# A gated recurrence and a feed-forward on one core: TensorE's order written by hand, the recurrence one step ahead, first pairs turned on TensorE, the square on ScalarE

## The chip, the cores and the metric

One core of a Trainium2 chip. The metric is the device time of one execution in microseconds. A time is the median of a kernel's runs. A ratio is the mean time of one kernel's fast runs over the mean of the kernel before's fast runs in the same rounds, so it is not quite the ratio of the medians quoted beside it. The kernel before has 946.0 us (943.6 to 948.8, 3 runs), its profiled execution a span of 942.1 us.

## The reference, cut to what matters

```python
def _attn_ref(q, k, v, a_re, a_im):          # each 4 x 8 x 768 x 48
    mag = np.sqrt(a_re * a_re + a_im * a_im)
    scale = np.minimum(mag, 0.999) / (mag + 1e-06)
    a_re_n, a_im_n = (a_re * scale, a_im * scale)
    for t in range(S):
        ...                                   # complex state S, decayed by a at each t
        S_re, S_im = (new_re + kv, new_im)
        y[:, :, t] = np.einsum('bhd,bhde->bhe', q[:, :, t], S_re)
    return y

def _moe_ref(x, w_in, w_out):                 # 3072 x 384, 384 x 2048, 2048 x 384
    h = x @ w_in
    g = h * (1.0 / (1.0 + np.exp(-h)))
    return (g @ w_out).astype(np.float32)
```

The recurrence is done in 24 chunks of 128 time steps, two chunks (a pair) at a time: 12 pairs. Within a chunk, decays and phases are prefix sums, q and k are rotated by them, and one masked product of q and k gives attention weights. Each pair then goes through the feed-forward: eight *hidden* steps (12 matrix products each) and eight *result* steps (8 each). The feed-forward's weights arrive as pairs of 32-bit words, from which the kernel rebuilds fp32 values, piece by piece.

Some words used below. A *hole* is time in which TensorE stands. The *carry* is the last phase of the chunk before, added to the first row of a chunk's phases. *Gates* are the decays and phases made from `a_re` and `a_im`; a *burst* is a run of ScalarE functions of one kind for them (logarithms, or sines and arctangents, or exponentials), opened by a table load of 1.28 us. *Gating* is VectorE's product (L420) that follows ScalarE's tanh after a hidden step. The *front* is the time in which weights are still being rebuilt, the *steady part* what follows.

## The kernel before

The parts that matter: the rebuilding of a piece of weights, the making of the phases, and the order. A list of work for the recurrence, one for the gates ahead and one for the feed-forward are merged evenly, and a scheduler then chooses each engine's order within that.

```python
    def load_w(dst, parts):                 # one piece: 512 columns of w_in, 384 of w_out
        ...                                 # x, t, u: scratch tiles; lo, hi: the raw words
        nc.gpsimd.tensor_tensor(out=x, in0=hi.bitcast(F32), in1=hi.bitcast(F32), op=ALU.mult)
        nc.vector.tensor_scalar(out=t, in0=hi, scalar1=3, ...)
        nc.vector.scalar_tensor_tensor(out=t, in0=hi, scalar=-0x40000000, in1=t, ...)
        ...                                 # four more VectorE operations; the last writes dst

    def phases(n):
        ...
        if place(n)[1] > 0:
            carry = att.tile([1, DM], F32, tag="carry", name=f"carry{n}", bufs=1)
            nc.sync.dma_start(out=carry, in_=X[before(n)]["turn"][C - 1:C])
            nc.gpsimd.tensor_tensor(out=th[0:1], in0=th[0:1], in1=carry, op=ALU.add)
        ps = p_m.tile([C, DM], F32, tag="m", name=f"phase{n}")
        nc.tensor.matmul(ps, lhsT=upto, rhs=th, start=True, stop=True)
        ...

    def turned(n):                          # q and k to head-dimension-first
        ...
        nc.vector.transpose(sq, ...)        # 32x32 blocks
        for b in range(NB):
            for a in range(NA):
                nc.sync.dma_start(out=x["T"][ts(b, Q), :, a], in_=sq[ts(a, Q), b])
        ...

    for p in range(NP + 1):
        lists = []
        if p < NP:
            lists += [attention(p), ahead(p)]
        if p == 0:
            lists.append([... all pieces of w_in ...] + [... all pieces of w_out ...])
        else:
            lists.append(feed(p - 1))
        merge(*lists)
```

## Time and profile before

| What | Before |
|---|---|
| Median time, span of the profiled run | 946.0 us, 942.1 us |
| Mean granted TensorE clock in it | 0.856 |
| TensorE busy up to 300 us | 135.6 us |
| Start of the first attention weights, of the first result step | 60.6 us, 185.6 us |

The page of the kernel before has the engines' busy times in its first part and, in its fifth, the costliest groups (columns: line, engine, operation, tile; busy us and mean ns of one; idle us of the engine just before them and what ended most of it):

```profile
PE 702.8 (75%) x3424; PEld 518.6 (55%) x3424; DVE 431.4 (46%) x587; ACT 264.2 (28%) x409; POOL 161.5 (17%) x144
...
L398 PE MATMUL o<-w,g 128*128 128x384 f32 x768 | 283.4, 515 | 16.1 <-DVE g L388 16.1
...
L321 PE MATMUL a<-T 96*128 96x128 f32 x384 | 57.8, 301 | 74.7 <-DMA T<-sq 74.7
L254 PE MATMUL phase<-th,upto 128*128 128x384 f32 x48 | 31.2, 755 | 99.4 <-POOL th L252 63.9
```

TensorE is the busiest engine but stands for a quarter of the span. It stands at two places above all: 75 us at attention weights, for turned q and k, and 99 us at the phase sums, mostly for the carry that GpSimd adds.

### The profile page before, as it was taken

How to read it: one execution, taken by the hardware profiler on the slowest of the kernel's cores; microseconds unless marked ns; L12 is line 12 of the kernel's file. 1: busy time of each engine (PE TensorE's matmuls, PEld its weight loads, DVE VectorE, ACT ScalarE, POOL GpSimd, SP SyncE). 2: the span in 40 equal slices, each digit the busy share in tenths (PEclk: the TensorE clock that was granted, in tenths of full speed). 3: DMA queues.
4: the chain of work that ended last, by engine and by line, in shares of the span. 5: the costliest groups of instructions: out<-in, count | busy, mean ns of one | idle time of the engine just before them, and what ended most of it. 6: DMA issues, size and time to landing. Idle time of an engine off the chain costs nothing.

```text
span 942.1 us, 9656 instructions
## 1 busy us (share of the span) xinstructions
PE 702.8 (75%) x3424; PEld 518.6 (55%) x3424; DVE 431.4 (46%) x587; ACT 264.2 (28%) x409; POOL 161.5 (17%) x144
## 2 busy tenths in 40 slices
PE   0333002855988979969979939979979859999997
PEld 0133001643765756746757727757757637777675
DVE  2856998896335244264362153362362252331110
ACT  5641000142161260251341251341521341311111
POOL 1411222232022031040040040040120040100000
PEclk9655555886997978989979969979979969999999
DMA  9335346744224313422602632612532522222000
GB/s 141 71 65 102 91 115 138 172 113 73 43 48 67 71 35 50 87 37 35 111 10 44 113 60 36 110 17 39 92 45 37 95 44 51 37 50 39 3 17 20
DMA packets 309592, 61.83 MB, mean 66 GB/s; under 512 B 300552, under 2 KB 305952, under 8 KB 309536
## 3 DMA queue, kind: packets, MB, share of 16 engines
q1 hardware_dynamic: 309536, 61.14, 35.3%
q8 instruction: 29, 0.48, 0.2%
q14 instruction: 27, 0.22, 0.1%
HBM read 36.25 MB, written 4.76 MB: 44 GB/s over the span
## 4 chain that ended last, share of the span: by engine, by line
PE 57%; DVE 12%; ACT 12%; SPq 5%; issue 5%; POOL 4%; DMA 3%; DVEq 0%; POOLq 0%; ACTq 0%
PE o L398 25%; PE h L383 22%; ACT mag L192 3%; ACT s L192 3%; ACT L189 3%; PE a L321 2%; POOL mag L222 2%; PE s L366 2%; SPq L312 2%; PE y L341 2%; DVE qk L298 2%; ACT cs L192 2%; DVE t L151 2%; PE phase L254 1%; PE y L344 1%
## 5 line engine op out<-in xcount | busy, mean ns | idle before, releaser
L398 PE MATMUL o<-w,g 128*128 128x384 f32 x768 | 283.4, 515 | 16.1 <-DVE g L388 16.1
L383 PE MATMUL h<-xT,w 128*128 128x256 f32 x1152 | 264.6, 381 | 3.1 <-DMA xT<-y 3.1
L383 PEld LDWEIGHTS h<-xT,w 128*128 128x128 f32 x1152 | 217.0, 191 | 46.3 <-issue 8.0
L398 PEld LDWEIGHTS o<-w,g 128*128 128x128 f32 x768 | 152.8, 201 | 119.0 <-DVE g L388 25.7
L388 DVE SCALAR_TENSOR_TENSOR g<-tanh,h 128x512 f32<-128x512 f32 x96 | 65.7, 684 | 253.1 <-ACT tanh L192 253.1
L192 ACT ACTIVATE tanh<-h 128x512 f32<-128x512 f32 x96 | 56.1, 594 | 383.3 <-PE h L383 374.2
L321 PE MATMUL a<-T 96*128 96x128 f32 x384 | 57.8, 301 | 74.7 <-DMA T<-sq 74.7
L254 PE MATMUL phase<-th,upto 128*128 128x384 f32 x48 | 31.2, 755 | 99.4 <-POOL th L252 63.9
L321 PEld LDWEIGHTS a<-T 96*128 96x128 f32 x384 | 55.4, 214 | 84.2 <-issue 61.3
L254 PEld LDWEIGHTS phase<-th,upto 128*128 128x128 f32 x48 | 11.3, 270 | 103.6 <-POOL th L252 65.7
L350 ACT COPY xT<-y 128x384 f32<-128x384 f32 x24 | 11.4, 475 | 175.1 <-PE y L341 107.3
L372 POOL TENSOR_TENSOR S<-S,decs 96x384 f32<-96x384 f32 x16 | 13.2, 825 | 273.4 <-DVE S L371 212.0
L325 DVE TENSOR_TENSOR w<-a,upto 128x512 f32<-128x512 f32 x48 | 32.3, 681 | 59.1 <-PE a L321 59.1
L366 PE MATMUL s<-v,qk 128*96 128x48 f32 x320 | 38.3, 281 | 26.6 <-ACT y L352 18.3
L366 PEld LDWEIGHTS s<-v,qk 128*96 128x96 f32 x320 | 37.1, 198 | 32.2 <-ACT y L352 19.7
L222 POOL TENSOR_TENSOR mag<-mag,s 128x768 f32<-128x768 f32 x12 | 25.2, 2100 | 163.8 <-DVE s L202 151.1
L341 PE MATMUL y<-w,v 128*64 128x128 f32 (+1 forms) x384 | 42.2, 294 | 13.1 <-DVE w L325 13.1
L189 ACT ACT_TABLE_LOAD x37 | 47.5, 1283 | 1.4 <-PEq L620 0.8
L148 POOL TENSOR_TENSOR x<-raw 128x384 f32<-128x384 f32 (+1 forms) x28 | 27.7, 988 | 99.2 <-DVE w L159 69.1
L192 ACT ACTIVATE mag<-mag 128x768 f32<-128x768 f32 x36 | 30.2, 838 | 46.9 <-POOL mag L222 46.0
L308 DVE STREAM_TRANSPOSE sq<-qk 128x1536 f32<-128x1536 f32 x24 | 42.4, 1766 | 2.1 <-DMA T<-sq 2.1
L298 DVE TENSOR_TENSOR qk<-ek,cs 128x768 f32<-128x768 f32 x24 | 38.0, 1582 | 9.6 <-POOL ek L296 9.6
(51 smaller groups left out, 613.2 us busy)
## 6 DMA issues: line engine op xcount, KB each, us to landing
T<-sq SPq DMA_DIRECT2D x288, 64.0 KB
raw<-in_moe_w_out_dram SPq DMA_DIRECT2D x16, 384.0 KB
re<-in_a_re_dram SPq DMA_DIRECT2D x24, 192.0 KB
im<-in_a_im_dram SPq DMA_DIRECT2D x24, 192.0 KB
k<-in_k_dram SPq DMA_DIRECT2D x24, 192.0 KB
q<-in_q_dram SPq DMA_DIRECT2D x24, 192.0 KB
v<-in_v_dram SPq DMA_DIRECT2D x24, 192.0 KB
raw<-in_moe_w_in_dram SPq DMA_DIRECT2D x24, 192.0 KB
```

What stands on the lines that cost most here:

```text
L189: chain(nc.scalar.preload_act_table_set(name))
L192: chain(nc.scalar.activation(out=out, in_=in_, func=func, **kw))
L222: nc.gpsimd.tensor_tensor(out=mag, in0=mag, in1=s1, op=ALU.add)
L254: nc.tensor.matmul(ps, lhsT=upto, rhs=th, start=True, stop=True)
L298: nc.vector.tensor_tensor(out=x["qk"][:, w], in0=heads(e).unsqueeze(2).to_broadcast([C, H, 2, D]), in1=x["cs"], op=ALU.mult)
L308: nc.vector.transpose(sq, x["qk"].rearrange("p w h c d -> p (w h) (c d)").rearrange("p g (b i) -> p b g i", i=Q))
L321: nc.tensor.matmul(ps[:, h], lhsT=x["kT"][:, hh * HH + h], rhs=x["qT"][:, hh * HH + h], start=True, stop=True)
L341: nc.tensor.matmul(to, lhsT=v_[:, cols], rhs=x["w", h // HH][:, h % HH], start=True, stop=not carried)
L366: nc.tensor.matmul(ps[:, h], lhsT=x["qk"][:, 1, h].rearrange("p c d -> p (c d)"), rhs=x["v"][:, h], start=True, stop=True)
L383: nc.tensor.matmul(ps[:, ji], lhsT=w1[:, dc, ts(jp * 2 + ji, C)], rhs=A[p]["xT"][:, dc], start=(dc == 0), stop=(dc == ND - 1))
L388: nc.vector.scalar_tensor_tensor(out=g, in0=th, scalar=1.0, in1=ps, op0=ALU.add, op1=ALU.mult)
L398: nc.tensor.matmul(A[p]["o"][m], lhsT=A[p]["g", jp][:, ji, ts(m, C)], rhs=w2[:, j], start=(j == 0), stop=(j == NJ - 1))
```

## The change

Its intent: fill TensorE's holes. The square leaves GpSimd. The first two pairs' q and k are turned by TensorE and need no transfers. While weights are still being rebuilt, two feed-forwards run side by side, so that each new piece is used twice. And after the front every pair's phase sums are issued a whole step before they are needed. All of TensorE's instructions stand in the order in which the program names them. Smaller parts came with it: a third buffer for raw words, the first loads of q, k and v issued by ScalarE, the first pair's gates in halves, and the PSUM buffers shared in another way.

```diff
-        nc.gpsimd.tensor_tensor(out=x, in0=hi.bitcast(F32), in1=hi.bitcast(F32), op=ALU.mult)
+        nc.scalar.activation(out=x, in_=hi.bitcast(F32), func=AF.Square)
@@ gates: the first pair in halves, on VectorE
+        helper = nc.vector if split else nc.gpsimd
@@ rotated
-            nc.gpsimd.tensor_tensor(out=e, in0=x[name].rearrange("p h d -> p (h d)"), in1=e,
-                                    op=ALU.mult)
+            (nc.vector if n < EARLY else nc.gpsimd).tensor_tensor(
+                out=e, in0=x[w].rearrange("p h d -> p (h d)"), in1=e, op=ALU.mult)
@@ turned
+        if n < EARLY:
+            for g in range(4):
+                w, hh = divmod(g, 2)
+                ps = p_o.tile([D2, HH, C], F32, tag="o", name=f"tp{n}_{g}")
+                for h in range(HH):
+                    nc.tensor.transpose(
+                        ps[:, h],
+                        x["kq"[w] + "r"][:, hh * HH + h].rearrange("p c d -> p (c d)"), ident)
+                nc.scalar.copy(out=T[:, ts(g, HH)], in_=ps)
@@ PSUM: weights, output, state and sums share two buffers
-    p_a = fast.enter_context(tc.tile_pool(name="p_a", bufs=2, space=PSUM))
-    p_o = fast.enter_context(tc.tile_pool(name="p_o", bufs=2, space=PSUM))
+    p_o = fast.enter_context(tc.tile_pool(name="p_o", bufs=4, space=PSUM))
@@ order of the pieces of weights (1: w_in, 2: w_out)
+    conv = [(1, s, lambda s=s, dc=dc: load_w1(s, dc)) for s in range(2) for dc in range(ND)]
+    for s in range(4):
+        conv += [(2, j // 2, lambda j=j: load_w2(j)) for j in range(4 * s, 4 * s + 4)]
+        if s < 2:
+            conv += [(1, s + 2, lambda s=s, dc=dc: load_w1(s + 2, dc)) for dc in range(ND)]
@@ the order: h(p), r(p) are hidden and result steps of pair p
+    with tc.manual_schedule(engines={mybir.EngineType.PE}):
+        angles(0, True)
+        both(phases, 0)
+        ... (the front, some 110 lines, by hand)
+        for p in range(3, NP + 1):
+            step(p, parts(hidden, p - 1), parts(result, p - 1))
@@ the steady step, cut
+    def step(p, h, r):
+        ...
+        h(1)
+        if ahead:
+            both(phases, p + 1)
+        h(1)
+        ...
+        weights(2 * p, 0); weights(2 * p, 1)
+        r(1)
+        state(2 * p); output(2 * p)
+        ...
+        trig_burst(p + 1)
+        ...
```

## The prediction

> **What bounds the kernel now.** I read the busy digits first, then busy time by stretch, TensorE's waits, and last the chain of waits. The digits (a slice is 23.6 us):
>
> ```profile
> span 942.1 us, 9656 instructions
> ...
> PE   0333002855988979969979939979979859999997
> ...
> DVE  2856998896335244264362153362362252331110
> ...
> PEclk9655555886997978989979969979979969999999
> ```
>
> In slices 3 to 6 VectorE reads 6 to 9 while TensorE reads 0 to 3 at half clock. From slice 11 TensorE reads 9, with a dip about every third slice. Busy time by stretch (columns: length; busy us and count of PE, PEld, DVE, ACT, POOL; clock, DMA share, GB/s):
>
> ```profile
> 80.00:120.00 40.00, 6.33 (x33) 5.47 (x32) 31.19 (x43) 0.65 (x2) 9.75 (x9) 0.50 0.55 116
> 120.00:160.00 40.00, 5.40 (x18) 3.99 (x18) 35.29 (x56) 0.00 (x0) 9.40 (x10) 0.50 0.53 126
> ...
> 650.00:710.00 60.00, 53.25 (x249) 39.79 (x248) 25.02 (x31) 20.81 (x33) 11.38 (x10) 0.89 0.35 62
> ...
> 770.00:830.00 60.00, 60.00 (x289) 44.84 (x288) 23.04 (x30) 14.32 (x26) 4.12 (x5) 1.00 0.29 49
> ```
>
> Three regimes: a front where VectorE is the bound (78 to 88% busy, mostly rebuilding weights from raw words), a middle where TensorE has holes, an end where TensorE is 100% busy at full clock. TensorE's waits (total us, times, longest), in the first 225 us:
>
> ```profile
> PE a L321 <- DMA T<-sq: 74.7, 4, 52.4
> PE phase L254 <- DVE th L238: 35.5, 2, 22.8
> ```
>
> and after 220 us:
>
> ```profile
> PE phase L254 <- POOL th L252: 43.2, 5, 14.1
> PE s L366 <- ACT y L352: 16.8, 4, 5.2
> PE o L398 <- DVE g L388: 16.1, 9, 3.6
> ```
>
> In the front TensorE waits for turned q and k, whose making queues behind the weights. Later it stands, in order, at a phase or state product whose input or buffer is late, with feed-forward work that needs neither queued behind. The chain of waits shows what a hole costs (start, us, what):
>
> ```profile
> 690.60 0.20 issue
> ...
> 692.50 5.49 PE o L398 x8
> 697.99 2.96 PE h L383 x12
> ```
>
> The eight result products took 5.49 us right after a hole; with TensorE kept busy they take 2.58.
>
> **What the Trainium skill says.** (1) "TensorE: Matmul & The Clock Gate", Part 1: TensorE's clock falls to half after an idle window of about 3.4 us and returns after as long of work. The trace agrees: 5.49 against 2.58 us. (2) "SBUF — State Buffer", Who interferes with whom: a VectorE instruction with two SBUF inputs contends with a GpSimd one that reads SBUF. It agrees: while GpSimd squares the raw words, the weight step with two SBUF inputs (L151, 128x512) takes 1.41 us; free of it, 0.69. (3) "ScalarE: Activation LUTs", What ACT_TABLE_LOAD costs: 1283 ns plus a drain of about 1380. The trace shows 1283 (37 times), but the next activation starts 0.02 us after a load (33.70 + 1.28, then 35.00), so I charge 1.28 only. (4) "VectorE: DVE Perf Modes", The three transpose paths: VectorE turns 32x32 blocks only, TensorE whole tiles but into PSUM. Hence the 12 transfers after each block transpose, which took SyncE 8.24 us to issue.
>
> **Full-clock cost of TensorE's work**, from the dense end: a hidden step (12 products) 2.59 us, a result step (8) 2.58, attention weights of one chunk (16) 1.79, its output (32) 1.8, its state (16 for a pair) 1.5, a phase or decay sum 0.65. Per pair: 8 x 2.59 + 8 x 2.58 = 41.3; 2 x (1.79 + 1.8) + 1.5 + 4 x 0.65 = 11.3; together 52.6. Twelve pairs: 631 us, the floor. In the middle the first result step of a pair starts at 287.1, and seven pairs later at 767.2: 68.6 us per pair, 16 over the floor. The waits after 220 us sum to 79 us; the rest is mostly half-clock work after them.
>
> **The change part by part.** *Weights.* Per 512-column piece VectorE spends 0.42 + 0.69 + 0.43 + 3 x 0.69 = 3.6 us free of GpSimd (4.49 from piece to piece at 105 us); per 384-column piece 2.9 (3.61). The square moves to ScalarE, 0.5 to 0.6 us each, about 15 us in all on an engine that is 28% busy. 12 x 3.6 + 16 x 2.9 = 90 us, where the groups now sum to 109. About 19 us gained on the engine that bounds the front.
>
> *First pairs.* Four block transposes (1.77 us each, 7 us) leave VectorE and their 48 transfers leave the queue; 64 TensorE transposes and 16 ScalarE copies come (about 0.5 us each, from the 128x384 copy's 475 ns). But VectorE takes over from GpSimd 8 products of q or k (0.55 each) and 4 half-size ones for the first gates (2.2 us): roughly even. The 52.4 us wait goes. Starting the first pair in halves with VectorE for GpSimd (2.1 + 1.8 us in its chain) gains about 5 us, but six loads issued first on ScalarE, near 1 us each as on SyncE, hold up its first square. Net 1 to 2: first phase at 21 us instead of 22.8.
>
> *The front's length.* I sum VectorE's new order at these durations. It ends the first pair's rotations near 35 us. The second pair follows a latency chain (log, GpSimd, arctan, sum, sine, exp, rotation) to about 76. At the first result step of pair 0, VectorE has 75 us of work behind it and the clock reads about 92. From there to the masking of chunk 4's attention weights lie 87 us of work. Walking TensorE beside it, I find about 5 us of waits at the third pair's gates, 3.5 at the hidden steps of pair 1, 2 at its phase sums, and 3 scattered: 92 + 87 + 14 = about 193. In that time TensorE does 12 hidden and 13 result steps (67 us) of two feed-forwards, so one VectorE stretch feeds twice the TensorE work.
>
> *What is left at 193 us.* Two hidden and three result steps 12.9; attention of chunks 4 and 5, 8.8; sums 2.6; ten feed-forwards 414; attention of nine pairs, less what first and last pairs lack, 96. Sum 534 us.
>
> *Holes left.* At the hand-over to the steady order, pair 3 has only 8 or 9 us of TensorE work between its trigonometric burst and its weights. The burst needs two table loads, sines, arctan, exponentials (8 us), GpSimd's products (4), rotation and transpose (3), 12 transfers (10): I expect 15 to 18 us of wait, once. In the steady order this chain, about 24 us, starts after the fourth hidden step of the pair and has some 32 us of TensorE work in front: hidden, with 8 us to spare. The phase input now comes a step ahead. So I count 8 us for all steady holes instead of 16 per pair.
>
> *Sum.* 193 + 534 + 18 + 8 + 6 (last product to end, 936.3 to 942.1 now) = 759; call it **760 us**. As a check from the other side: at 223 us the old kernel still had about 606 us of full-clock work and took 719. The new one gains 30 us of clock and 72 us of work by the front's end, and 113 - 26 = 87 in the steady part: 189 of 946.
>
> **The rivals.** (a) *The steady chain isn't hidden.* Weights of both chunks, state, output and sums now share two PSUM buffers where weights had two of their own, and a late ScalarE copy behind a table burst would stop TensorE. For: the state's wait on ScalarE's y copy already costs 16.8 us. Against: in the new order a result step lies between weights and state and a hidden step between output and sums, 2.6 us against a copy of 0.5. If it comes true at 5 us a pair plus half clock, 60 to 70 us: 825. (b) *The front stays as long.* VectorE obeys in-order waits on ScalarE, which now also squares and copies; with another 25 us of stalls the time is 785. For: ScalarE's order puts log bursts between tanh and copies. Against: it has about 100 us of work in 190. (c) *The raw-word transfers become the bound of the front:* 12.3 MB in about 150 us is 82 GB/s. Against: the page reaches 172 GB/s in a slice, and VectorE waited only 1.4 us for raw words with two buffers (three now). Worth 10 us at most. (d) *Better than I think:* the hand-over hole is filled and front waits are half: 735.
>
> **Range and chances.** TensorE's 534 us are measured rates times counted work; the uncertainty is the front (plus or minus 20) and holes (minus 15 to plus 50), so it leans upward: 728 to 800. Losing all 189 us would need the front and steady estimates both to fail: faster 0.97, same 0.02, slower 0.01.
>
> **What would show it.** The weight step L151 had 1.39 us at the median between 88 and 170 us: its successor should take 0.69 (512 columns) and 0.55 (384). First attention weights before 40 us (60.6 now); VectorE near 90% busy from 95 to 195 us, TensorE about 70%. Weights all converted by about 200 us. From 245 us TensorE over 95% busy at a clock near 1.0 and 53 to 54 us per pair; no GpSimd wait at the phase sum. One wait of TensorE for turned q and k, near 15 us, around 225 to 245 us. I am wrong if pairs still take 60 us or more, or the weights end after 220 us.

## The result, and the profile after

The changed kernel takes **826.1 us** (825.4 to 826.6, 4 runs) against 944.8 us (943.1 to 948.8, 4 runs) in the same rounds: ratio 0.874, 95% interval 0.871 to 0.877. Faster by far, and 26 us past the upper end of the predicted range. From the page of the changed kernel:

```profile
span 824.0 us, 9608 instructions
...
PE 701.7 (85%) x3488; PEld 524.2 (64%) x3488; DVE 430.0 (52%) x622; ACT 300.4 (36%) x470; POOL 131.8 (16%) x108
...
PE   0586468908896599999999999899999899999997
...
DVE  2858858796556635653663565526436613521110
...
PEclk9768779867897699999999999899999899999999
```

TensorE's busy time is what it was (702 us). Only its holes went. A slice is 20.6 us. From the fifteenth slice (288 us) its digits are 9, with two 8s and the end. In front of that, after 124 us, there are two gaps: the ninth slice (165 to 185 us) reads 0, the thirteenth and fourteenth (247 to 288 us) 6 and 5, with a clock of 6 to 7 tenths in all three. TensorE's waits over the whole span (us in total, times, longest) say what they are:

```profile
PE o L430 <- DVE w L154: 47.3, 10, 19.9
PE phase L270 <- DVE th L249: 23.2, 2, 22.3
PE a L352 <- DMA T<-sq: 9.1, 1, 9.1
```

After 300 us the list is short; its two largest entries are:

```profile
PE s L399 <- DVE w L356: 5.8, 2, 2.9
PE a L352 <- DVE turn L274: 2.2, 5, 0.7
```

So of the 186 us of waits that the prediction showed (74.7 + 35.5 + 43.2 + 16.8 + 16.1) for the old kernel, the 74.7 us for turned q and k are 9.1, and the 43.2 us for GpSimd's carry are gone from the steady part. In their place stand 47.3 us in which a result step waits for its piece of weights (L154 writes it). This wait is new. Busy time by stretch (columns as in the prediction), from the first result step to chunk 4's attention weights, and over two steady pairs:

```profile
97.00:222.50 125.50, 83.54 (x257) 54.55 (x258) 92.02 (x156) 38.19 (x57) 17.90 (x12) 0.77 0.48 105
```

```profile
332.42:443.91 111.49, 109.82 (x593) 83.74 (x592) 61.20 (x74) 46.72 (x70) 26.26 (x20) 1.00 0.39 68
```

In the front VectorE, the engine that I took for the bound, is busy 92.0 of 125.5 us and TensorE 83.5: neither is busy throughout, they wait for each other. In the steady part TensorE is busy 98.5% of the time at full clock, and a pair still takes 111.49 / 2 = 55.7 us.

How two engines come to wait for each other is to be seen in the trace between 146 and 155 us (start, length, engine, work, idle before):

```profile
146.03 4.21 PE L430 MATMUL o<-w,g 128*128 128x384 f32 x6 [1.55 <-DVE w L154]
...
150.03 3.76 PE L416 MATMUL h<-xT,w 128*128 128x256 f32 x12
150.14 0.56 DVE L154 SCALAR_TENSOR_TENSOR w<-x,w 128x384 f32<-128x384 f32 x1
...
153.83 0.60 ACT L189 ACTIVATE g<-h 128x512 f32<-128x512 f32 x1 [4.66 <-PE h L416]
...
154.46 0.69 DVE L420 SCALAR_TENSOR_TENSOR g<-g,h 128x512 f32<-128x512 f32 x1 [3.76 <-ACT g L189]
```

TensorE had stood for a piece of weights. When it came, TensorE did the result step, then the hidden step behind it, both slowly (six products of a result step in 4.00 us, where eight take 2.58 when TensorE is kept busy). VectorE meanwhile reached the gating of that hidden step (L420), which stands in its order ahead of the next piece, and stood 3.76 us for it. Then the next piece is late in its turn. Seven such waits of VectorE between 97 and 222.5 us add up to 24.9 us.

The longest wait of TensorE, 19.86 us up to 186.57, has another look. Its piece is the first of the last eight of `w_out`, and in VectorE's order there stand ahead of it three pieces of `w_in` that TensorE needs only five steps later, the gates of pair 3 and rotations of pair 2. Some of that work is stretched beside GpSimd:

```profile
186.57 1.65 PE L430 MATMUL o<-w,g 128*128 128x384 f32 x2 [19.86 <-DVE w L154]
...
162.04 2.19 POOL L227 TENSOR_TENSOR mag<-mag,s 128x768 f32<-128x768 f32 x1 [51.90 <-DVE s L199]
...
162.47 2.04 DVE L144 TENSOR_SCALAR w<-raw 128x512 int32<-128x512 int32 x1
```

The same operation takes 0.42 us at 155.06, where GpSimd is idle. The piece was not all that was late there. The result step also needs the gating of a hidden step that ended at 161.54; its tanh started only at 174.29, 12.7 us later, because it stands in ScalarE's order behind the bursts of pairs 3 and 2, and the gating ended at 181.64. So with the piece at hand TensorE would still have stood until about 181.6.

At the hand-over to the steady order, TensorE's line of the trace has four holes, 2.26 + 1.82 + 2.89 + 9.10 = 16.1 us, and slow steps after three of them (a hidden step takes 4.93 and 4.17 us, not 2.59; the clock reads 0.66 from 253.3 to 258.2, 0.62 from 263.8 to 269.4 and 0.57 from 278.5 to 286.3):

```profile
253.25 4.93 PE L416 MATMUL h<-xT,w 128*128 128x256 f32 x12 [2.26 <-DMA xT<-y]
260.00 0.91 PE L270 MATMUL phase<-th,upto 128*128 128x384 f32 x2 [1.82 <-POOL th L262]
263.81 1.65 PE L270 MATMUL phase<-th,upto 128*128 128x384 f32 x2 [2.89 <-POOL th L262]
265.25 4.17 PE L416 MATMUL h<-xT,w 128*128 128x256 f32 x12
278.52 3.75 PE L352 MATMUL a<-T 96*128 96x128 f32 x16 [9.10 <-DMA T<-sq]
282.06 4.29 PE L430 MATMUL o<-w,g 128*128 128x384 f32 x8
```

### The profile page after: what moved, and what is told of

Its sections match the earlier page's. It is cut to its first block, busy times and chain, and to the rows that moved or that the text cites. A ratio compares the mean times of both kernels' runs of the same rounds, so it can differ in the third digit from the quotient of the medians.

```text
span 824.0 us, 9608 instructions
## 1 busy us (share of the span) xinstructions
PE 701.7 (85%) x3488; PEld 524.2 (64%) x3488; DVE 430.0 (52%) x622; ACT 300.4 (36%) x470; POOL 131.8 (16%) x108
## 4 chain that ended last, share of the span: by engine, by line
PE 60%; DVE 13%; issue 12%; ACT 7%; DMA 2%; POOL 2%; SPq 2%; ACTq 1%; DVEq 0%; POOLq 0%
PE o L430 25%; PE h L416 23%; PE a L352 3%; PE y L372 2%; PE s L399 2%; PE y L375 2%; DVE sq L339 2%; ACT L186 2%; PE L L291 2%; ACT mag L189 1%; DVE qr L318 1%; PE phase L270 1%; ACT cs L189 1%; POOL mag L227 1%; DMA raw<-in_moe_w_in_dram 1%
## 5 line engine op out<-in xcount | busy, mean ns | idle before, releaser
L430 PE MATMUL o<-w,g 128*128 128x384 f32 x768 | 275.5, 507 | 48.0 <-DVE w L154 47.3
L420 DVE SCALAR_TENSOR_TENSOR g<-g,h 128x512 f32<-128x512 f32 x96 | 65.5, 682 | 276.3 <-ACT g L189 276.0
L189 ACT ACTIVATE g<-h 128x512 f32<-128x512 f32 x96 | 57.2, 597 | 312.9 <-PE h L416 312.9
L318 DVE TENSOR_TENSOR kr<-L,cs 128x768 f32<-128x768 f32 x24 | 41.9, 1769 | 14.4 <-POOL L L314 14.3
L270 PE MATMUL phase<-th,upto 128*128 128x384 f32 x48 | 21.4, 572 | 27.9 <-DVE th L249 23.2
L314 POOL TENSOR_TENSOR L<-k,L 128x384 f32<-128x384 f32 x20 | 20.9, 1061 | 129.6 <-ACT L L189 102.0
L399 PEld LDWEIGHTS s<-v,kr 128*96 128x96 f32 x320 | 33.4, 182 | 11.3 <-DVE w L356 7.4
L399 PE MATMUL s<-v,kr 128*96 128x48 f32 x320 | 33.8, 264 | 6.0 <-DVE w L356 6.0
L189 ACT ACTIVATE mag<-mag 128x768 f32<-128x768 f32 (+1 forms) x39 | 30.5, 789 | 23.1 <-POOL mag L227 21.0
L375 PE MATMUL y<-T,S 96*64 96x128 f32 x320 | 36.3, 287 | 0.0
L143 ACT ACTIVATE x<-raw 128x384 f32<-128x384 f32 (+1 forms) x28 | 17.0, 606 | 48.8 <-DVE w L154 45.0
```

Of the source, the lines that this page charges most:

```text
L189: chain(nc.scalar.activation(out=out, in_=in_, func=func, **kw))
L318: nc.vector.tensor_tensor(out=x[w + "r"], in0=heads(e).unsqueeze(2).to_broadcast([C, H, 2, D]), in1=x["cs"], op=ALU.mult)
L375: nc.tensor.matmul(to, lhsT=x["S"].rearrange("p h d -> p (h d)")[:, cols], rhs=x["qT"][:, h], start=False, stop=True)
L399: nc.tensor.matmul(ps[:, h], lhsT=x["kr"][:, h].rearrange("p c d -> p (c d)"), rhs=x["v"][:, h], start=True, stop=True)
L420: nc.vector.scalar_tensor_tensor(out=g, in0=g, scalar=1.0, in1=ps, op0=ALU.add, op1=ALU.mult)
L430: nc.tensor.matmul(A[p]["o"][m], lhsT=A[p]["g", jp][:, ji, ts(m, C)], rhs=w2[:, j], start=(j == 0), stop=(j == NJ - 1))
```

## The experiments

Theory, after reading the two traces: the front is long because TensorE's and VectorE's fixed orders disagree about the pieces of weights, and GpSimd's work beside VectorE lengthens it. Rivals: VectorE has simply too much to rebuild; the two side-by-side feed-forwards or the hand order itself cost what they should gain; or the missing time is in the steady part, where GpSimd and buffers still hold TensorE.

To tell front from rest in each run I use a marker: the start of the phase sums of pair 3, the last thing before the steady order. In the changed kernel it is at 233.6 us, and 590.4 us remain to the end of the span. The third column is the ratio to the kernel before of the same session, the fourth that ratio over 0.8738, less 1, times 826 us (the interval of each ratio is 0.003 to 0.005 either way, so each is good to some 3 to 5 us).

| Run | Median us | Ratio | Against the change, us | Marker, us | Rest, us |
|---|---|---|---|---|---|
| the change | 826.1 | 0.874 | | 233.6 | 590.4 |
| e1 square back on GpSimd | 833.7 | 0.880 | +6 | 240.2 | 589.8 |
| e2 no turning on TensorE | 854.8 | 0.902 | +27 | 261.8 | 590.3 |
| e3 scheduler's order | 851.5 | 0.899 | +24 | | |
| e4 before, square on ScalarE | 933.2 | 0.985 | | | |
| e5 no rebuilding (wrong result) | 798.3 | 0.843 | -29 | 205.7 | 587.2 |
| e6 no GpSimd products in front | 808.8 | 0.854 | -19 | 216.5 | 590.2 |
| e7 four more chunks turned on TensorE | 816.2 | 0.862 | -11 | 223.5 | 590.5 |
| e8 one feed-forward after the other | 822.6 | 0.868 | -6 | 233.5 | 589.0 |
| e9 phase sums not a step ahead | 875.9 | 0.925 | +48 | 232.7 | 641.8 |
| e10 pieces in order of need | 815.4 | 0.862 | -11 | 223.4 | 590.1 |
| e11 e10 and e6 | 802.3 | 0.848 | -25 | 211.2 | 589.6 |
| e12 e10, e7, GpSimd later still | 789.1 | 0.833 | -39 | 197.3 | 590.9 |

All but e5 are correct. The rest is 587 to 591 us in every run with a marker but e9 (e3 leaves TensorE's order to the scheduler and has no such border, e4 is the old kernel): front and steady part don't touch each other, so the two errors of the prediction can be taken one at a time.

### e4 and e1: the square alone, and all but the square

```diff
# e4: the kernel before with
-        nc.gpsimd.tensor_tensor(out=x, in0=hi.bitcast(F32), in1=hi.bitcast(F32), op=ALU.mult)
+        nc.scalar.activation(out=x, in_=hi.bitcast(F32), func=AF.Square)
# e1: the changed kernel with these two lines the other way round
```

> One part alone: the old kernel with the square on ScalarE. Theory A (VectorE's rebuild sets the front's end there): 12 to 19 us faster than 945, so 926 to 933. Rival (TensorE's waits for turned q and k set it, the rebuild hidden): under 5 us.

> Undoes one part: the square of the raw words goes back to GpSimd. 28 squares lengthen the weight step with two SBUF inputs by about 0.7 us (512 columns) or 0.5 us (384) each, some 17 us of VectorE. Theory A (VectorE and TensorE wait for each other in turn, and each rebuilt piece lies on that path): 10 to 17 us slower than 826, so 836 to 843. Theory B (VectorE's 33 us of idle time between 97 and 222 us is slack that takes it up): under 4 us slower.

Measured: 933.2 us against 948.6 in e4's session, ratio 0.985 (interval 0.981 to 0.989), a gain of 14 us: clear of the noise, and inside the first expectation. In e4 the weight step L151 has a median of 0.56 us (1.06 before): the step was slow because of GpSimd's square, as the prediction read it. Taking the square back in the changed kernel costs only 6 to 8 us: there VectorE idles 33.5 of the 125.5 us above, and the other half of the expected cost may fall into that, which no run tests. This lies between the two expectations.

### e2: TensorE's turning of the first pairs

```diff
-    EARLY = 4
+    EARLY = 0
```

> Undoes one part: no TensorE transposes, the first four chunks are turned by VectorE blocks and transfers and their products are on GpSimd again. If the early start of the first pairs carries the gain of the front: 30 us or more slower (856 or more), with one wait of TensorE for turned q and k of 15 us or more. If the front is set by the weight rebuild in any case (first result step at 97 us because the second weight matrix is late): under 10 us slower.

Measured: 27 us slower, a little under the 30 of the first expectation, all of it before the marker. The waits of TensorE for turned q and k come back:

```profile
PE a L352 <- DMA T<-sq: 30.9, 4, 13.1
PE a L352 <- DMA k<-in_k_dram: 23.6, 1, 23.6
```

`EARLY` also moves these chunks' products of q and k back to GpSimd, so the run does not separate the two.

### e3: the order by hand

```diff
-    with tc.manual_schedule(engines={mybir.EngineType.PE}):
+    if True:
```

> Undoes one part: TensorE's order is left to the scheduler, everything else as in the changed kernel. If the hand order fills the steady holes: 8 to 14 us more per pair over eight pairs, so 890 to 940. If the gain comes from the other parts (work emitted a step ahead): within 15 us of 826.

Measured: 851.5 us, 24 us slower: between the two expectations, far below the first and 10 us over the second. The hand order is worth its time only in the steady part. With the scheduler, TensorE has done 221.8 us of work by 300 us (193.6 by hand), because it passes over a result step whose piece is late (14.2 us of waits at result steps for pieces instead of 47.3). But after 300 us its waits are larger than the two entries shown for the changed kernel:

```profile
PE h L416 <- DVE g L420: 21.2, 6, 4.0
PE h L416 <- DMA xT<-y: 15.0, 9, 3.1
```

and pairs take about 65 us (from phase sum to phase sum) instead of 57.

### e9: the phase sums not a step ahead

```diff
 def step(p, h, r):
-        if ahead:
-            both(phases, p + 1)
 ...
         trig_burst(p + 1)
+        if p + 2 < NP:
+            both(phases, p + 2)
 ...
         trig_burst(3)
+        both(phases, 4)
```

> Undoes one part in the steady order (from pair 3 on): the phase sums of the next pair stand in TensorE's order right after the burst that makes their input, as in the old kernel, in place of a step later. If the step ahead fills the old holes: TensorE waits there for GpSimd's phase input each time, 8 to 12 us a pair with the half clock, over 8 pairs: 890 to 920. If the rest of the hand order had already filled them: within 10 us of 826.

Measured: 875.9 us, somewhat less than expected, and all of it in the rest: 641.8 instead of 590.4 us. The wait of the old kernel is back at nearly its old size (43.2 us there after 220 us):

```profile
PE phase L270 <- POOL th L262: 44.9, 12, 11.5
```

Pairs take about 63 us. Of the parts that were taken out alone, the step ahead is the largest: about 50 us of the 119.

### e5: no rebuilding of weights

```diff
-        nc.scalar.activation(out=x, in_=hi.bitcast(F32), func=AF.Square)
-        nc.vector.tensor_scalar(out=t, in0=hi, scalar1=3, scalar2=0x3FFFFFF8,
+        nc.vector.tensor_scalar(out=t, in0=hi, scalar1=3, scalar2=0x3F7FFFF8,
                                 op0=ALU.logical_shift_left, op1=ALU.bitwise_and)
-        ...                      # the five other VectorE operations
```

> Wrong result on purpose: one VectorE operation per piece in place of six, and no square; all transfers and TensorE's order stay. 5/6 of 90 us, some 75 us, leaves VectorE in the front. Theory A (rebuild on the path of the alternating waits): the 47 us of TensorE waits for rebuilt weights go, 35 to 55 us faster, 771 to 791. Rival C (the latency chain of gates, turning and order in the first 97 us, or the transfers, set the front): under 20 us faster.

Measured: 29 us faster, between the expectations. One VectorE operation per piece is left of six, and VectorE's busy time between 97 and 180 us falls from 63.2 to 29.7 us. Yet TensorE still waits for pieces (the one operation left is at L143):

```profile
PE o L418 <- DVE w L143: 34.5, 5, 15.8
```

More than half of VectorE's work is away and 34.5 of 47.3 us of wait are left. From the first result step to chunk 4's masking VectorE is busy 40.1 of 110.4 us. So the amount of work is not what makes most of that wait. In its longest, 15.8 us up to 164.75, VectorE does gates of pair 3 and rotations of pair 2 ahead of the piece and stands 3.1 us for an arctangent and 3.3 us for a product of GpSimd: it is where the piece stands in VectorE's order, behind work that waits for others.

### e10: the pieces in the order in which TensorE asks for them

```diff
-    conv = [(1, s, ...) for s in range(2) for dc in range(ND)]
-    for s in range(4):
-        conv += [(2, j // 2, ...) for j in range(4 * s, 4 * s + 4)]
-        if s < 2:
-            conv += [(1, s + 2, ...) for dc in range(ND)]
+    conv = []
+    for s, js in enumerate(((0, 2), (2, 8), (8, 12), (12, 16))):
+        conv += [(1, s, lambda s=s, dc=dc: load_w1(s, dc)) for dc in range(ND)]
+        conv += [(2, j // 2, lambda j=j: load_w2(j)) for j in range(*js)]
```

> The changed kernel with one thing different: the weight pieces are rebuilt in the order in which TensorE's order asks for them (three pieces of the first matrix were put ahead of two pieces of the second that are asked for first, three times). If that order makes TensorE's waits for rebuilt weights (47 us, one of 19.9): these waits fall to 30 us or less and the time by 8 to 18 us, 808 to 818. If VectorE's total work before the last piece sets the end of the front: within 4 us.

Measured: 815.4 us, as expected; the marker is 10 us earlier. TensorE's waits at a piece and at the gating are now

```profile
PE o L430 <- DVE w L154: 14.7, 4, 7.8
PE o L430 <- DVE g L420: 14.1, 4, 13.5
PE h L416 <- DVE w L154: 13.7, 4, 6.3
```

The 19.9 us wait is gone. But the sum is still 42.5 us: a part has moved to the gating and to hidden steps. Right pieces first is worth 11 us and does not end the mutual waiting. The longest of these waits, 13.5 us, stands where the 19.9 us stood:

```profile
150.44 2.75 PE L416 MATMUL h<-xT,w 128*128 128x256 f32 x12
...
169.34 1.06 ACT L189 ACTIVATE g<-h 128x512 f32<-128x512 f32 x2
...
171.85 4.84 PE L430 MATMUL o<-w,g 128*128 128x384 f32 x8 [13.48 <-DVE g L420]
```

The piece is there, but the tanh of that hidden step starts 16 us after its end, behind the bursts of pairs 3 and 2 and squares of raw words. A third fixed order, ScalarE's, makes this wait; no run moves the tanh ahead of the bursts.

### e6 and e11: no GpSimd products in the front, alone and with e10

```diff
-        helper = nc.vector if split else nc.gpsimd
+        helper = nc.vector if p < 4 else nc.gpsimd
@@
-            (nc.vector if n < EARLY else nc.gpsimd).tensor_tensor(
+            (nc.vector if n < 6 else nc.gpsimd).tensor_tensor(
```

> GpSimd's gate products of pairs 1 to 3 and its q and k products of pair 2 go to VectorE: 6 times 0.96 and 4 times 0.55, 8 us more VectorE work, but no VectorE instruction is stretched by GpSimd before 200 us. If the stretching (about 8 us between 160 and 190 us, where single weight steps took 2.0 in place of 0.42 us, plus the 4.6 us GpSimd add near 95 us in the chain) costs on the path: 5 to 15 us faster. If only the in-order waits matter: within 4 us, or slower by up to 8.

> Order of need, and GpSimd's products of the front on VectorE. If the two causes are separate terms of the front: the sum of the 17 us seen without GpSimd and what the order alone brings, so about 795 if the order brings 12. If they are the same wait counted twice: 805 to 809.

Measured: e6 is 17 to 19 us faster than the change, a little over what was expected, although VectorE has more to do. It can gain by work that GpSimd no longer stretches and by a shorter gate chain; how much by each, and by which of the two edits, this run does not tell. In the trace, 7.7 us of it come before the first result step (89.3 instead of 97.0), 1.9 from VectorE's busy time up to chunk 4's masking (90.2 instead of 92.1, with more operations) and 7.5 from its idle time there (27.6 instead of 35.1). e11 is 25 us faster than the change, where e6 and e10 alone sum to 30. That lies between its two expectations: mostly separate causes, with some 5 us counted twice.

### e8: one feed-forward after the other

```diff
 def h(p):
-        feeds[p][0](1)
+        feeds[taken[0] // (NJ // 2)][0](1)
+        taken[0] += 1
 # r(p) likewise with taken[1]
```

> Undoes one part: the first two feed-forwards one after the other at the same places in TensorE's order. A piece of rebuilt weights then releases 2.6 us of TensorE work in place of 5.2 while the rebuild runs. If side by side matters as I predicted: 20 to 40 us slower, with TensorE's waits for rebuilt weights growing by as much. If only the total of VectorE's work before the last piece matters: under 8 us.

Measured: 822.6 us. Not slower but, if anything, a little faster. The marker stands where it stood (233.5). Running two feed-forwards side by side brings nothing in this front, against what the prediction said of it and what I expected before this run.

### e7: more chunks turned on TensorE

```diff
-    EARLY = 4
+    EARLY = 8
-                ps = p_o.tile([D2, HH, C], F32, tag="o", name=f"tp{n}_{g}")
+                ps = (p_o if n < 4 else p_m).tile([D2, HH, C], F32, tag="o" if n < 4 else "m", ...)
 # turned(n) of chunks 4 to 7 moved to just ahead of their attention weights
```

> A version meant to be better: chunks 4 to 7 too are turned by TensorE through the shared PSUM buffers, their products on VectorE, placed in TensorE's order just before their weights. Takes away the wait for turned q and k at 278 us (9 us plus about 8 us of half clock and phase waits around it) and GpSimd's stretching near 175 us. 10 to 25 us faster, 801 to 816. Rival: ScalarE's copies and TensorE's extra transposes (64 more, about 8 us) give it back: within 5 us.

Measured: 11 us faster, but not where it was expected. The 9.1 us wait for transfers at the hand-over is gone, yet the rest takes 590.5 us as before. TensorE now has 48 transposes to do there (about 6 us, estimated from 1.05 us for eight in the changed kernel's trace) and waits for the copies:

```profile
PE a L352 <- ACT T L335: 3.8, 5, 1.3
```

The gain is in front of the marker (223.5 us). There the edit also takes the products of these chunks from GpSimd, as e6 does for two of them, so the gain may be that. The expectation failed in its place and cause.

### e12: what helped, together

e10, e7, and the gates on VectorE for pairs 0 to 4.

> A version meant to beat both: order of need, no GpSimd in the front (gates of pairs 1 to 4, products of chunks 0 to 7 on VectorE), chunks 0 to 7 turned by TensorE. If the three gains add: 780 to 795. If more VectorE work in the front gives part back: 795 to 808.

Measured: **789.1 us** (783.3 to 792.1), ratio 0.833, with a correct result: 39 us better than the change and faster than both kernels. The marker is at 197.3 us, so the front is 36 us shorter, and the rest is 590.9. From the first result step to chunk 4's masking VectorE is now busy 92.2 of 104.1 us: with the orders put right, it comes near to the bound that the prediction took it for. What is left of TensorE's waits for pieces:

```profile
PE h L416 <- DVE w L154: 10.4, 4, 5.1
...
PE o L430 <- DVE w L154: 7.2, 2, 6.8
```

One wait of 9.0 us for a gating is left too, with its tanh 10.6 us behind its hidden step.

## Why the prediction was right and wrong

**Right: the direction, and what the old kernel lost its time to.** The old kernel lost its time in TensorE's holes, and the change fills them. e9 shows that the step ahead ends the wait for the carry, e2 that turning the first pairs on TensorE, with their products on VectorE, ends the wait for transfers, e4 that the weight step was slow because of GpSimd. The checks named ahead: no carry wait in the steady part (true but for two at the hand-over, 4.7 us), the weight step at 0.55 us free of GpSimd (median 0.56), TensorE over 95% busy from 245 us (95.4% from 245 to 818 us, but 70.5% up to 300, where the hand-over lies, and 98.1% after). One wait for turned q and k at the hand-over (9.1 us at 278.5, expected 15 at 225 to 245). Missed: first attention weights before 40 us (42.5); from 95 to 195 us VectorE 80% and TensorE 60% busy (90 and 70 expected); pairs of 57.4 us (53 to 54); and the weights, all rebuilt at 240.5 us instead of about 200. With this last one a sign came true that the prediction itself had named for being wrong, weights that end after 220 us.

**Wrong: the size.** By its sum the time should have been 759 us; the profiled span is 824.0, so 65 us are to be accounted for. The prediction set chunk 4's masking at 193 us; it starts at 224.2. So 31 us are lost in the front, and 34 in what follows: 599.8 us instead of 759 - 193 = 566.

*The front: "75 us of work behind it and the clock reads about 92", "87 us of work", "14" of waits.* The start was 97 (+5), with 67.3 us of work behind it, the work from there 92.0 in place of 87 (+5), the waits, up to the masking, 127.2 - 92.0 = 35.2 in place of 14 (+21). Together the 31. So the sum of VectorE's work was sound (67.3 + 92.0 = 159 us where 75 + 87 = 162 were expected) and the walk of TensorE beside it was not. This is the step that failed: I let a piece be ready when VectorE's work summed to it, and saw few of the places where VectorE stands at a gating for a hidden step that TensorE cannot reach. e10 shows that the order of pieces makes 10 us of the front, e6 that GpSimd's share makes 17; e11 takes out 22 together. The trace shows GpSimd's part directly too, in steps of 2.04 us that take 0.42 alone. The rival that the prediction named (b), VectorE in wait for ScalarE, 785, was half right. 24.9 us of VectorE's waits are for tanh, but in all seven the tanh started 0.04 us after its hidden step's end in the trace: there TensorE was late, not ScalarE. At the longest hole, though, ScalarE was late, by 12.7 us, behind bursts as (b) has it; what this alone costs is not shown. Rival (c), the raw words, is out: VectorE does not wait for them at all, and ScalarE's squares once, 3.9 us. And "one VectorE stretch feeds twice the TensorE work" was simply wrong: e8 does without it and loses nothing.

*The cost of a pair: "state (16 for a pair) 1.5", output 1.8.* Here I miscounted. Eight heads give 16 products in the profile's count for each **chunk**, and they take 341.58 to 342.99 = 1.41 us: 2.82 us a pair, not 1.5. A chunk's output takes 1.97, not 1.8. With sums of 0.645 a pair costs 41.36 + 2 x (1.79 + 1.97 + 1.41) + 2.58 = 54.3 us instead of 52.6. From chunk 4 on, 16 chunks have a state to keep (0.66 us more each, 10.6) and 20 an output (0.17 more each, 3.4): 14 of the 34 us.

*The hand-over: 18.* Measured 16.1 us of holes and about 7.6 us of slow work after them (4.93 + 4.17 + 3.75 + 4.29 = 17.1, where 2 x 2.59 + 1.79 + 2.58 = 9.5 is the full-clock time): 24. That the holes sum to what was expected is partly luck: the one wait foreseen, for turned q and k, took 9.1 us, and the other 7.0 are for the carry (4.7) and for transfers into xT (2.3), which were not foreseen. I had left out the slow work behind the holes, although the prediction itself had shown what it costs. 6 us.

*Steady holes: 8.* By subtraction (34 - 14 - 6) they are 22, 14 more. Six pairs in a row can be marked by their phase sums (332.42 to 677.10): 57.4 us each, 3.1 over the 54.3. Two of them hold the same hole of 2.90 us. One of the two, and the clock of TensorE in the stretches around it:

```profile
528.35 0.96 DVE L247 SCALAR_TENSOR_TENSOR mag<-re,mag 128x768 f32<-128x768 f32 x1 [3.31 <-ACT mag L189]
...
530.22 1.28 DVE L356 TENSOR_TENSOR w<-a,upto 128x512 f32<-128x512 f32 x2
...
530.96 1.36 PE L399 MATMUL s<-v,kr 128*96 128x48 f32 x7 [2.90 <-DVE w L356]
```

```profile
528.10:530.90 2.80, 0.00 (x0) 0.00 (x0) 2.51 (x4) 2.74 (x5) 0.05 (x1) 1.00 0.00 0
530.90:534.00 3.10, 3.04 (x20) 2.95 (x22) 2.71 (x4) 0.75 (x2) 1.91 (x2) 0.51 0.32 66
534.00:537.00 3.00, 3.00 (x31) 2.99 (x28) 1.82 (x3) 0.00 (x0) 1.10 (x2) 0.50 0.01 1
537.00:540.00 3.00, 3.00 (x15) 2.38 (x12) 1.34 (x1) 0.65 (x2) 2.58 (x3) 0.87 0.03 7
```

VectorE stands for an arctangent, the masking of the attention weights stands behind it in VectorE's order, and with it the PSUM buffer that the state needs. The hole of 2.9 us drops the clock to half for the next 6 us, and so costs about 6.2 in all: the state's 16 products take 2.72 us from start to start (1.41 at full clock), the output 3.67 (1.97), the hidden step 2.88 (2.59). That is close to the mechanism of rival (a), which named 825 us: late work behind a table burst that keeps a shared PSUM buffer, though VectorE's masking here and not a copy of ScalarE. But the sum is not its: it foresaw 5 us a pair, and the two holes together are 5.8 us. The total agreed with it by chance. The other four of the six pairs are 1.3 to 2.0 us over 54.3, in small gaps that no single wait explains.

Three readings in the prediction are off without moving its sum. "Slices 3 to 6" holds only when slices are counted from 0. 12 hidden and 13 result steps are 64.6 us at its own rates, not 67. And its slow result step of 5.49 us follows a hole of 1.96 us that found the clock at 0.50 already; the longer hole, 4.78 us, had ended at 686.33.

**What stays open.** What e6 gains by which engine's relief; what a tanh ahead of ScalarE's bursts would bring in the front; whether a hand order with e12's pieces could also have the scheduler's freedom to pass over a late step, which e3 shows to be worth something in the front; and how far the two steady holes could be closed by a masking ahead of the arctangent, which no run tried.

## What to carry to other kernels

When engines obey fixed orders and feed each other, the time of a stretch is not the busiest engine's work plus a few waits: walk all the orders together (here TensorE's, VectorE's and ScalarE's), item by item, and check that things are made in the order in which they are asked for. Put a price on a hole that includes the half-clock work behind it: 2.9 us of hole cost 6.2 here. And when a cost is taken from the profile "per pair" or "per chunk", count the instructions in the trace against the program once.

## What the Trainium skill lacked or had wrong

- "TensorE: Matmul & The Clock Gate", Part 1, gives an idle window of about 3.4 us before the clock falls. A hole of 2.90 us between products after 13 us of dense work was enough here: the clock read 0.51 in the 3.1 us after it and 0.50 in the next 3.0, and the same again at 647.29. TensorE's weight loads stood 3.51 us there, so the window may count those; the page doesn't say. Part 4 of the same page times a transpose in bf16 only: eight in fp32 of 128x96 took 1.91 us at clock 0.50 and 1.08 us at 1.00.
- "ScalarE: Activation LUTs", What ACT_TABLE_LOAD costs, adds a drain of about 1380 ns to each load. Neither kernel shows it: in the changed one a load of 1.28 us starts at 154.44 and the next activation at 155.74.
- "SBUF — State Buffer", Who interferes with whom, has the rule of blocking, which the traces bear out (0.42 us free, 2.04 us beside a GpSimd addition of 2.19), but no page says what it comes to in a kernel: taking GpSimd's products out of the front gave 17 us, though VectorE then had more to do. How much of that is the blocking is not shown.
- No page treats engines with in-order queues that make each other wait. It was the largest error here: 35.2 us of VectorE's waits where 14 were expected, 26.3 with the pieces in order of need (e10) and 11.9 in e12.
